# Gated linear attention on one core: the outputs of the last two heads go into spare rows of the output tiles

## The chip, the core and the metric

The kernel runs on one core of a Trainium2 chip. That core has a matrix engine (TensorE, PE in the profile; PEld is its weight load), a vector engine (VectorE, DVE), an activation engine (ScalarE, ACT), a general engine (GpSimd, POOL), and a queue engine (SyncE, SP) that in this kernel issues almost all transfers. Operands lie in SBUF, a memory of 128 partitions; the matrix engine writes to PSUM, of which this kernel uses eight banks of 128 x 512 fp32 in its later part. Inputs, outputs and spilled data lie in HBM. The metric is the device time of one execution in microseconds (us), less being better.

## What is computed

The reference, cut to what matters (2048 tokens, width 640, 32 heads of 20 features, a feed-forward width of 1536; all fp32):

```python
xn = _layernorm(x)
q, k, v = heads(xn @ wqkv)                       # 32 heads, 20 features each
phi = lambda t: concat(softmax(t @ w_phi), softmax(-(t @ w_phi)))    # 40 per head
kv = einsum("bhsf,bhsd->bhfd", phi(k), v)        # a 40 x 20 state for each head
z = einsum("bhsf->bhf", phi(k))
o = (phi(q) @ kv) / (phi(q) @ z + 1e-6)
s = o.reshape(B, S, D) @ wo
g = silu(gelu(xn @ w1 + b1) @ w2 + b2)
return x + s * g
```

## The kernel before

**Stages.** A first stage projects keys and values and sums up the state `kv`, then projects the queries. A second stage runs the feed-forward part in 12 units. A third stage, at the end, is the one that the change touches: for each of four chunks of 512 tokens (loop over `ORDER = (2, 3, 0, 1)`) it makes the attention output `o`, multiplies it by `wo`, multiplies by the gate, adds the residual and stores the result. In the second and third stage the order of the instructions on every engine is the order of the code (`manual_schedule`).

**Precision.** A large product is done in three passes on split operands (`PASSES`): a value is kept as a high part, written by ScalarE, and the low remainder, written by VectorE; high x high, high x low and low x high are added up. So a tile of outputs `oT[0][j]` has the shape 128 x 2 x 512, high part first.

**Rows of the output tiles.** Thirty heads have 600 features, which lie in five tiles `oT[0][0..4]` of 128 rows: each tile holds two groups of 60 features in 64 rows, so that 4 of every 64 rows are spare and hold zeros (`bdk`, the block-diagonal state, has 64 columns of which 60 are used). The last two heads have 40 more features. They have a tile of their own, `oT[1]`: `bdl` holds their state three times side by side (120 columns), so that one product makes three copies in 120 rows; VectorE subtracts the high part from one copy by a column of factors (`lowsel`), and `load_wol` builds a matching 120-row weight `wol` (with `midsel`). So all three passes of these 40 features are one product of 120 rows.

**Three functions of a chunk.**
- `num_t` transposes `phi(q)` of 256 tokens (half `p` of the chunk) for one tile `j` into `ph`; `j` = 5 stands for the last two heads.
- `num_m` multiplies `ph` by `bdk` or `bdl` in fp32 (two column halves of the array, each its own instruction) and splits the result into `oT`. `num_groups` does the 12 pairs (`j`, `p`) in groups of four (of three for the first chunk): transposes of a group, then the products of the group before it, then a `yield`.
- `finish(c, d, ...)` makes 128 columns (`d` = 0 to 4) of the result for a chunk: 15 products of 512 columns from `oT[0]` and a sixteenth from `oT[1]`, then the gate on VectorE and the residual sum on GpSimd (on VectorE for the last two), both in halves of 256, then the store.

**Order.** In the loop over `d`, `load_res` issues the loads of residual `xres` and gate `gt` two steps ahead, `finish` comes next, then a step of `late_q` (head sums and scaling of four query tiles, those of the chunk that comes last, each ending in a store to `phi_dram`), then one group of the next chunk's `num_groups`. So the next chunk's `oT` is made between the `finish` steps of this one: groups of transposes and products after `d` = 0, 1, 2, the last products after `d` = 3, nothing after `d` = 4. All loads and stores go through SP, which issues them in order and waits at each for what that one needs. `load_phi` loads four tiles of 640 KB; the one for the third chunk stands after `d` = 0 of the first, the one for the fourth after `d` = 3 of the second.

Of the kernel before, what the change touches and what calls it, by code (L numbers as in the profile page):

```python
# [8 lines left out]
F32 = mybir.dt.float32  # L9
F32R = mybir.dt.float32r  # L10
# [5 lines left out]
P = 128  # L16
# [29 lines left out]
def hedgehog_gated_mlp_kernel(ctx: ExitStack, tc: tile.TileContext, x, xt_in, wqk, bd, wv, wo, w1, b1, w2, b2, out_t):  # L46
# [62 lines left out]
    for h in range(3):  # L109
# [4 lines left out]
    lowsel = const.tile([P, 1], F32, name="lowsel")  # L114
    nc.gpsimd.memset(lowsel[:], -1.0)
    nc.gpsimd.affine_select(out=lowsel[:], in_=lowsel[:], pattern=[[0, 1]],
                            compare_op=OP.is_ge, fill=0.0, base=-80, channel_multiplier=1)
    midsel = const.tile([P, 1], F32, name="midsel")
    nc.gpsimd.memset(midsel[:], -1.0)
    nc.gpsimd.affine_select(out=midsel[:], in_=midsel[:], pattern=[[0, 1]],  # L120
                            compare_op=OP.is_ge, fill=0.0, base=-40, channel_multiplier=1)
    nc.gpsimd.affine_select(out=midsel[:], in_=midsel[:], pattern=[[0, 1]],
                            compare_op=OP.is_ge, fill=0.0, base=79, channel_multiplier=-1)
    const.tile([P, 8], F32, name="align")
    bdk = const.tile([P, 10, 64], F32, name="bdk")
    bdl = const.tile([P, 120], F32, name="bdl")
# [436 lines left out]
    def kv_rest():  # L563
        kv_acc(NT - 1, phis.pop(NT - 1), vs.pop(NT - 1))
        kvr = const.tile([P, 360], F32, name="kvr")
# [7 lines left out]
    def kv_state(kvr):  # L573
        nc.gpsimd.memset(bdk[:, :, 60:], 0.0)
        ps = bankB()
        for g, m in enumerate((P, P, 96)):
            nc.tensor.transpose(ps[:120, g * P:g * P + m], kvr[:m, 120 * g:120 * g + 120], ident[:m, :m])
        s3 = ps[:120, :320].rearrange("p (f r) -> p f r", r=32)
        nc.vector.tensor_tensor(bdk[:120, :, :60].rearrange("p f (h d) -> p f h d", d=20),
                                s3[:, :, None, :20].to_broadcast([120, 10, 3, 20]),  # L580
                                mask[:120, None, :, None].to_broadcast([120, 10, 3, 20]), op=OP.mult)
        for r in range(3):
            nc.vector.tensor_tensor(bdl[:80, 40 * r:40 * r + 40].rearrange("p (h d) -> p h d", d=20),
                                    ps[:80, None, 320:340].to_broadcast([80, 2, 20]),
                                    mask[:80, :2, None].to_broadcast([80, 2, 20]), op=OP.mult)
# [95 lines left out]

    def q_load(t):
        e = slab(F32, "eq")
        ef = e[:].rearrange("p a b -> p (a b)")
        nc.sync.dma_start(ef, e_dram[t])
        return ef

    def q_norm(t, ef):
# [19 lines left out]
        nc.sync.dma_start(phi_dram[t], ef)  # L708

    def load_wol():  # L710
        raw = row([P, D], F32, "raw")
        for r in range(3):
# [338 lines left out]
```

## Time and profile before

| what | value |
|---|---|
| time, median of 3 runs | 686.34 us (686.0 to 686.5) |
| the profiled execution's own time | 688.63 us |
| its span on the core | 686.9 us |
| granted TensorE clock in that span | 0.999 |
| instructions | 11941 |
| HBM read, written | 79.85 MB, 45.10 MB |

The span is the time from the first to the last instruction on the core; the execution's own time has some 1.7 us around it. Profiled and unprofiled executions differ a little, so a sum that is made on the profiled one is set against the median as a difference. In the rows below, L804 is line 804 of the kernel before; a name such as `pB<-oT,wo` says what is written from what, with buffer numbers left out. A matrix instruction in fp32 shows as two records, one in the format of the split operands as one. `busy` of matrix instructions overlaps, since they are pipelined: the distance between starts is what one costs in a row of them, and the view of the chain of work that ended last is cut at such starts.

### The profile page before, as it was taken

The numbers are of one execution on the slowest core, as the hardware profiler recorded it, in microseconds if no ns is written. First come the engines' busy times: TensorE is split into PE (matmuls) and PEld (weight loads), VectorE is DVE, ScalarE is ACT, GpSimd is POOL, SyncE is SP. The second block draws the span as 40 slices with busy tenths as digits, with TensorE's granted clock in tenths as the row PEclk, the third lists the DMA queues.
The fourth block names the chain that finished last, engine by engine and source line by source line (L and its number), as shares of the span: only waits on it lengthen the run. The fifth ranks groups of instructions, "written<-read, shape, count | busy, mean of one in ns | idle before, by whom it ended". The sixth has DMA issues, their size and how long they took to land.

```text
span 686.9 us, 11941 instructions
## 1 busy us (share of the span) xinstructions
PE 676.7 (99%) x4713; PEld 590.6 (86%) x4713; DVE 455.5 (66%) x730; ACT 251.3 (37%) x398; POOL 375.6 (55%) x336
## 2 busy tenths in 40 slices
PE   8899999999999999999999999999999999999997
PEld 8899999999999998888887888888888887777875
DVE  4788566886876456677978774676977655774232
ACT  3332313323332237244353347633233354425430
POOL 1355244859577355866968853636456640783221
PEclk9999999999999999999999999999999999999999
DMA  9820052734261153329687697376364491886623
GB/s 339 305 88 2 3 150 81 242 79 149 51 216 59 80 171 134 115 70 329 211 301 260 210 421 319 90 266 240 140 206 153 145 396 49 314 295 210 231 93 107
DMA packets 73966, 125.73 MB, mean 183 GB/s; under 512 B 5694, under 2 KB 42558, under 8 KB 73014
## 3 DMA queue, kind: packets, MB, share of 16 engines
q1 hardware_dynamic: 71606, 114.48, 48.9%
q10 hardware_dynamic: 2304, 10.49, 4.2%
q8 instruction: 37, 0.61, 0.4%
q14 instruction: 19, 0.16, 0.1%
HBM read 79.85 MB, written 45.10 MB: 182 GB/s over the span
## 4 chain that ended last, share of the span: by engine, by line
PE 90%; DVE 5%; ACT 1%; issue 1%; DMA 1%; POOL 1%; SPq 0%; DVEq 0%; POOLq 0%; ACTq 0%
PE pA L306 30%; PE pB L645 22%; PE pB L616 18%; PE pB L804 11%; PE pB L746 3%; PE pB L735 2%; PE kv L377 2%; PE pA L163 2%; DVE y L654 2%; DVE xhi L670 1%; DMA xt<-in_x_dram 1%; PE pA L292 1%; PE pB L753 1%; DVE rc L340 0%; PE pB L590 0%
## 5 line engine op out<-in xcount | busy, mean ns | idle before, releaser
L645 PE MATMUL pB<-hs,w2s 128*128 128x512 f32 x720 | 167.1, 390 | 0.0
L645 PEld LDWEIGHTS pB<-hs,w2s 128*128 128x128 f32 x720 | 134.7, 188 | 29.2 <-PE pB L746 0.8
L616 PE MATMUL pB<-xp,w1s 128*128 128x512 f32 x324 | 81.4, 390 | 1.0 <-DVE pB L888 1.0
L616 PE MATMUL pB<-xd,w1s 128*128 128x512 f32 x324 | 79.3, 389 | 0.0
L332 ACT ACTIVATE e<-e 128x1280 f32<-128x1280 f32 x32 | 40.7, 1272 | 91.5 <-POOL e L327 91.0
L804 PE MATMUL pB<-oT,wo 128*128 128x512 f32 x300 | 72.9, 394 | 0.0
L616 PEld LDWEIGHTS pB<-xp,w1s 128*128 128x128 f32 x324 | 60.7, 188 | 13.9 <-DVE pB L888 1.4
L654 DVE TENSOR_TENSOR y<-pB,y 128x512 f32<-128x512 f32 x100 | 63.9, 680 | 12.3 <-PE pB L645 12.1
L616 PEld LDWEIGHTS pB<-xd,w1s 128*128 128x128 f32 x324 | 60.8, 188 | 12.6
L804 PEld LDWEIGHTS pB<-oT,wo 128*128 128x128 f32 x300 | 55.4, 188 | 14.8 <-ACT ph L738 1.2
L345 POOL TENSOR_TENSOR e<-e,rc 128x1280 f32<-128x1280 f32 x16 | 39.0, 2440 | 48.5 <-DVE rc L365 48.2
L345 POOL TENSOR_TENSOR eq<-eq,rc 128x1280 f32<-128x1280 f32 x16 | 38.0, 2372 | 50.0 <-DVE rc L704 50.0
L327 POOL TENSOR_TENSOR e<-nr,e 128x640 f32<-128x640 f32 x32 | 45.4, 1421 | 33.5 <-DVE nr L326 30.7
L306 PE MATMUL pA<-wv,xp 128*128 128x320 f32 x384 | 61.0, 312 | 0.8 <-DVE nr L326 0.4
L621 ACT ACTIVATE pB<-pB,b1t 128x512 f32<-128x512 f32 x48 | 31.8, 662 | 77.3 <-DVE pB L888 28.4
L306 PE MATMUL pA<-wk,xp 128*128 128x320 f32 x384 | 59.9, 311 | 0.0
L306 PE MATMUL pA<-wq,xp 128*128 128x320 f32 x384 | 59.0, 309 | 0.0
L306 PEld LDWEIGHTS pA<-wv,xp 128*128 128x128 f32 x384 | 56.9, 188 | 1.7 <-issue 0.7
L306 PEld LDWEIGHTS pA<-wq,xp 128*128 128x128 f32 x384 | 56.9, 188 | 0.1
L306 PEld LDWEIGHTS pA<-wk,xp 128*128 128x128 f32 x384 | 56.8, 188 | 0.1
L691 POOL TENSOR_TENSOR ez<-eq,zrep 128x1280 f32<-128x1280 f32 x16 | 47.3, 2953 | 1.1 <-PE pB L753 1.1
L401 POOL TENSOR_TENSOR w1s<-raw,w1s 128x640 fp32r<-128x640 f32 (+1 forms) x18 | 25.7, 1429 | 36.8 <-ACT w1s L400 29.6
(139 smaller groups left out, 1046.0 us busy)
## 6 DMA issues: line engine op xcount, KB each, us to landing
raw<-in_w_dram SPq DMA_DIRECT2D x42, 320.0 KB, 4.4
e_dram<-e ACTq DMA_DIRECT2D x16, 640.0 KB, 3.3
eq<-e_dram SPq DMA_DIRECT2D x16, 640.0 KB, 6.9
phi_dram<-eq SPq DMA_DIRECT2D x16, 640.0 KB, 3.4
phi<-phi_dram SPq DMA_DIRECT2D x16, 640.0 KB, 9.5
xt<-in_x_dram SPq DMA_DIRECT2D x16, 320.0 KB, 4.8
xres<-in_xt_dram SPq DMA_DIRECT2D x20, 256.0 KB, 4.5
out_dram<-xres SPq DMA_DIRECT2D x18, 256.0 KB, 3.0
```

The lines of the kernel that those rows point to most:

```text
L306: nc.tensor.matmul(ps[:, hf, :HALF], stat_x(q, o, k, a), ws[k][:, b, hf * HALF:(hf + 1) * HALF], start=n == 0, stop=n == 3 * KC - 1)
L327: nc.gpsimd.tensor_tensor(e5[:, :, :, 1, :], nr[:, :, :, None].to_broadcast([P, 2, 16, DH]), e5[:, :, :, 0, :], op=OP.subtract)
L332: nc.scalar.activation(ef, ef, AF.Exp)
L345: nc.gpsimd.tensor_tensor(e3, e3, rc[:, :, None].to_broadcast([P, 64, DH]), op=OP.mult)
L401: nc.gpsimd.tensor_tensor(sl[:, 1, :n], src, sl[:, 0, :n].bitcast(F32), op=OP.subtract)
L616: nc.tensor.matmul(bank[ch][:], tl[:, a, off + wo_:off + wo_ + P], mov(blk, b), start=new and n == 0, stop=n == len(mms) - 1, skip_group_c ...
L621: nc.scalar.activation(ps, ps, AF.Gelu_apprx_tanh, bias=b1t[:, f:f + 1])
L645: nc.tensor.matmul(ps[:], ws[i][:, b, d * P:(d + 1) * P], hs[o][i][:, a, :], start=i == n == 0, stop=(i, n) == (GF - 1, 2), skip_group_che ...
L654: nc.vector.tensor_tensor(y, ps[:], y, op=OP.add)
L691: nc.gpsimd.tensor_tensor(zv, ef, zf, op=OP.mult)
L746: nc.tensor.matmul(po[64 * e:64 * e + 64, :256], bdk[:n, 2 * j + e, :], ph[:n, e * 256:(e + 1) * 256], start=True, stop=True)
L804: nc.tensor.matmul(ps[:], w, o, start=n == 0, stop=n == 15)
```

## The change

The 40 outputs of the last two heads are now moved into the 4 spare rows of every 64: rows 15, 31, 47, ... of each tile `oT[0][j]`, eight rows for each of the five tiles. `bdk`'s columns, and the rows of `wo` on the host, are put in the order that leaves every sixteenth row free, and `wo` has 640 rows in place of 680. `bdl` has 40 columns, made by one instruction; `lowsel`, `midsel` and `load_wol` are gone. A transfer from SBUF to SBUF (`spread`) copies eight rows of `oT[1]` (high and low part of 512 tokens, 4 KB a row) into `oT[0][j]` behind the products of the second half of `j`; to that end `j` = 5 is done first. `finish` has fifteen products. The residual sum of all steps is on VectorE, in one piece of 512 columns (halves in the last two steps). In the chunk loop, stores are collected and issued after the step's products (`put`, `put_all`), and the fourth chunk's `load_phi` stands after `d` = 2 of the second chunk.

```diff
-    bdl = const.tile([P, 120], F32, name="bdl")
+    bdl = const.tile([P, 40], F32, name="bdl")
...
-        nc.vector.tensor_tensor(bdk[:120, :, :60].rearrange("p f (h d) -> p f h d", d=20),
-                                s3[:, :, None, :20].to_broadcast([120, 10, 3, 20]),
-                                mask[:120, None, :, None].to_broadcast([120, 10, 3, 20]), op=OP.mult)
-        for r in range(3):
...
+        for h in range(3):
+            nc.vector.tensor_scalar(
+                bdk[:120].rearrange("p f (q c) -> p f q c", c=16)[:, :, :, 5 * h:5 * h + 5],
+                s3[:, :, :20].rearrange("p f (q i) -> p f q i", i=5), mask[:120, h:h + 1], None, op0=OP.mult)
...
+    stores, late_store = [], [False]
+
+    def put(dst, src):
+        if late_store[0]:
+            stores.append((dst, src))
+        else:
+            nc.sync.dma_start(dst, src)
+
+    def put_all():
+        while stores:
+            nc.sync.dma_start(*stores.pop(0))
...
-            for a, b in ((0, 64), (64, 120)):
-                nc.tensor.matmul(po[a:b, :256], bdl[:n, a:b], ph[:n, :256], start=True, stop=True)
+            nc.tensor.matmul(po[:40, :256], bdl[:n, :], ph[:n, :256], start=True, stop=True)
             o2 = oT[1]
...
+    def spread(j, oT):
+        nc.sync.dma_start(oT[0][j][15::16].bitcast(F32), oT[1][8 * j:8 * j + 8].bitcast(F32))
...
-        steps = [(j, p) for p in range(2) for j in range(6)]
+        steps = [(j, p) for p in range(2) for j in (5, 0, 1, 2, 3, 4)]
...
+                num_m(j, oT, p, n, ph)
+                if p and j < 5:
+                    spread(j, oT)
...
-        steps.append((wol[:120, d * P:(d + 1) * P], oT[1][:120, 1, :]))
         for n, (w, o) in enumerate(steps):
-            nc.tensor.matmul(ps[:], w, o, start=n == 0, stop=n == 15)
+            nc.tensor.matmul(ps[:], w, o, start=n == 0, stop=n == 14)
...
-        for o in range(2):
-            sl = slice(o * W2, (o + 1) * W2)
+        w = W2 if last else CW
+        for o in range(0, CW, w):
+            sl = slice(o, o + w)
...
-            (nc.vector if last else nc.gpsimd).tensor_tensor(xr[:, sl], g, xr[:, sl], op=OP.add)
+            nc.vector.tensor_tensor(xr[:, sl], g, xr[:, sl], op=OP.add)
...
-            nc.sync.dma_start(out_t[d * P:(d + 1) * P, c * CW:(c + 1) * CW], xr[:])
+            put(out_t[d * P:(d + 1) * P, c * CW:(c + 1) * CW], xr[:])
...
-    wol = load_wol()
...
             next(nxt, None)
-            if ci + 2 < NCH and d == (0 if ci == 0 else 3):
+            put_all()
+            if ci + 2 < NCH and d == 2 * ci:
                 phin = load_phi(ORDER[ci + 2])
```

What the change moves is seen best in the order of instructions on two engines. **SP, in the first chunk's steps `d` = 2 and 3**; first before (`out_0_dram` is the result, `eq` a query tile of `late_q`, `phi_dram` its store):

```order
L784 DMA xres_6064<-in_xt_dram 128x512
L788 DMA gt_6066<-g_dram_86 128x512
L814 DMA out_0_dram<-xres_5907 128x512
L708 DMA phi_dram_82<-eq_5935 128x1280
L784 DMA xres_6147<-in_xt_dram 128x512
L788 DMA gt_6149<-g_dram_86 128x512
L814 DMA out_0_dram<-xres_5984 128x512
L685 DMA eq_6173<-e_dram_81 128x1280
```

and the same place now:

```order
L781 DMA xres_6043<-in_xt_dram 128x512
L785 DMA gt_6045<-g_dram_86 128x512
L749 DMA oT_5889<-oTl_5894 8x1024
L683 DMA out_0_dram<-xres_5895 128x512
L781 DMA xres_6124<-in_xt_dram 128x512
L785 DMA gt_6126<-g_dram_86 128x512
L688 DMA eq_6146<-e_dram_81 128x1280
L749 DMA oT_5890<-oTl_5894 8x1024
L749 DMA oT_5891<-oTl_5894 8x1024
L749 DMA oT_5892<-oTl_5894 8x1024
L749 DMA oT_5893<-oTl_5894 8x1024
L683 DMA phi_dram_82<-eq_5919 128x1280
```

The small transfers of the next chunk's tiles (`oT<-oTl`) stand between loads and stores; four of them come in a row behind two loads and a query tile, and the store of the step's result stands behind them.

**SP, in the second chunk's steps `d` = 2 and 3**, before:

```order
L784 DMA xres_6379<-in_xt_dram 128x512
L788 DMA gt_6381<-g_dram_86 128x512
L814 DMA out_0_dram<-xres_6244 128x512
L784 DMA xres_6451<-in_xt_dram 128x512
L814 DMA out_0_dram<-xres_6306 128x512
L725 DMA phi_6496<-phi_dram_82 128x1280
L725 DMA phi_6497<-phi_dram_82 128x1280
```

and now:

```order
L785 DMA gt_6348<-g_dram_86 128x512
L749 DMA oT_6214<-oTl_6219 8x1024
L683 DMA out_0_dram<-xres_6220 128x512
L716 DMA phi_6417<-phi_dram_82 128x1280
L716 DMA phi_6418<-phi_dram_82 128x1280
L716 DMA phi_6419<-phi_dram_82 128x1280
L716 DMA phi_6420<-phi_dram_82 128x1280
L781 DMA xres_6425<-in_xt_dram 128x512
L749 DMA oT_6215<-oTl_6219 8x1024
L749 DMA oT_6216<-oTl_6219 8x1024
L749 DMA oT_6217<-oTl_6219 8x1024
L749 DMA oT_6218<-oTl_6219 8x1024
```

The four tiles of `phi` are now issued one step earlier, and the four small transfers stand right behind them.

**VectorE, around the last products of the first chunk's loop** (step `d` = 3; `rc` and `dn` are head sums of `late_q`), before:

```order
L809 TENSOR_TENSOR gt<-pB,gt 128x256 x2
L340 TENSOR_REDUCE rc<-eq 128x64
L694 RECIPROCAL rc<-rc 128x64
L750 TENSOR_TENSOR oT<-pB,oT 128x256 x3
L756 SCALAR_TENSOR_TENSOR oTl<-oTl,lowsel,pB 120x256
L340 TENSOR_REDUCE dn<-ez 128x64
```

and now:

```order
L806 TENSOR_TENSOR gt<-pB,gt 128x512
L807 TENSOR_TENSOR xres<-gt,xres 128x512
L330 TENSOR_REDUCE rc<-eq 128x64
L697 RECIPROCAL rc<-rc 128x64
L741 TENSOR_TENSOR oT<-pB,oT 128x256 x4
L330 TENSOR_REDUCE dn<-ez 128x64
```

The residual sum stands ahead of the head sum, and four low parts of `oT` follow behind it in place of three and the copy of the last two heads.

More of the change, by code (lines that the diff above doesn't have):

```diff
@@ L707, in q_norm @@
         yield
[L708 to L712, printed above, removed]
-            nc.sync.dma_start(raw[40 * r:40 * r + 40, :], wo[640:680, :])
-        wol_h = row([P, D], F32R, "wolh")
-        wol = row([P, D], F32R, "wol")
-        nc.vector.tensor_copy(wol_h[:120, :], raw[:120, :])
-        nc.vector.scalar_tensor_tensor(wol[:120, :], wol_h[:120, :].bitcast(F32), midsel[:120, :], raw[:120, :],
-                                       op0=OP.mult, op1=OP.add)
-        return wol
+        put(phi_dram[t], ef)
     def load_phi(c):
```

46 lines of the change are left out of this document (18 added, 28 removed).

## The prediction

> **What bounds the kernel now.** I read the page's busy times and its chain first, then the chain of the last 150 us in order of time, then the engines' busy times by stage.
>
> ```profile
> PE 676.7 (99%) x4713; PEld 590.6 (86%) x4713; DVE 455.5 (66%) x730; ACT 251.3 (37%) x398; POOL 375.6 (55%) x336
> PEclk9999999999999999999999999999999999999999
> PE 90%; DVE 5%; ACT 1%; issue 1%; DMA 1%; POOL 1%; SPq 0%; DVEq 0%; POOLq 0%; ACTq 0%
> ```
>
> The matrix engine is busy 99% of the span, at full clock in every slice, and 90% of the chain is its work. The change touches the third stage; of its chain from 540 us on I need the shares and these pieces (start, length, what):
>
> ```profile
> by line: PE pB L804 50.1%; PE pB L746 12.9%; PE pB L645 12.3%; PE pB L735 9.1%; PE pB L616 8.2%; PE pB L753 2.3%; DVE xres L810 0.6%; DVE y L809 0.5%; issue 0.1%; DVEq L809 0.0%
> ...
> 579.68 3.63 PE pB L804 x16
> ...
> 601.92 1.45 PE pB L746 x12
> 603.36 0.43 PE pB L753 x4
> 603.80 7.51 PE pB L804 x32
> ...
> 626.06 3.86 PE pB L804 x16
> ...
> 631.80 7.51 PE pB L804 x32
> ...
> 659.99 22.14 PE pB L804 x96
> ...
> 682.22 0.44 DVE y L809
> ```
>
> By the first row the chain from 540 us on has hardly an engine but PE, and what others have of it stands at the end: from 682 us the last gate and sum, then the store. What is taken off the matrix engine in this stage is gained, unless something then makes it wait.
>
> **The sixteenth product.** In the row of 659.99, 96 products of 512 columns take 22.14 us, back to back: 0.2306 us each. `finish` runs 20 times (4 chunks, 5 steps) and loses one product each time: 20 x 0.2306 = **4.61 us**, all on the path.
>
> **The halved product of the last two heads.** `num_m` with `j` = 5 runs 8 times (4 chunks, 2 token halves) and has one instruction of 40 columns in place of two of 64 and 56. To see what that is worth I need the price of such a record when it runs alone. L590 has fp32 records over the whole array:
>
> ```profile
> 267.84 2.15 PE pB L590 x8
> L590 PE MATMUL pB<-kvr,ident x8: 366/448/466, 267.7 to 269.6; 128*128 128x360 f32 x4, 128*128 128x320 f32 x2, 128*128 128x240 f32 x2
> ```
>
> 4 x 360 + 2 x 320 + 2 x 240 = 2560 columns in 2.15 us, or 0.215 us for 256 columns. The four records of L753 (two instructions, two records each) take 0.43 us, half of 4 x 0.215, so the two column halves run side by side. One instruction alone is then 2 x 0.215 = 0.43 us, as long as the pair. I take **0**. Were a record worth 0.108 us whatever stands beside it, two fewer would give 8 x 0.215 = 1.7 us; if the odd one also keeps its neighbours of L746 from pairing, up to as much is lost. The Trainium skill, "TensorEngine Tiling (Array Packing)", section Tiling Modes, says that different tiles of the array can run matrix instructions in parallel; by it nothing is saved here, without it 1.7 us, and the two rows agree with it.
>
> **VectorE and GpSimd.** 18 of the 20 steps change: two gate products of 256 on VectorE and two sums on GpSimd become one product and one sum of 512 on VectorE.
>
> ```profile
> L809 DVE TENSOR_TENSOR y<-pB,y 128x256 f32<-128x256 f32 x20 | 7.7, 420 | 29.5 <-PE pB L804 29.5
> L654 DVE TENSOR_TENSOR y<-pB,y 128x512 f32<-128x512 f32 x9 | 6.1, 690 | 2.5 <-PE pB L645 2.5
> L810 POOL TENSOR_TENSOR xres<-gt,xres 128x256 f32<-128x256 f32 x20 | 14.3, 737 | 27.7 <-DVE gt L809 22.5 <-issue 5.1
> 580.00:600.00 20.00, 20.00 (x132) 15.83 (x131) 12.52 (x24) 8.16 (x20) 12.38 (x9) 1.00 0.70 250
> 600.00:610.00 10.00, 10.00 (x52) 7.49 (x51) 8.55 (x19) 1.54 (x4) 7.67 (x6) 1.00 0.84 300
> 620.00:630.00 10.00, 10.00 (x62) 7.58 (x62) 3.52 (x11) 5.31 (x11) 4.57 (x5) 1.00 0.66 204
> ```
>
> GpSimd loses 36 x 0.737 = 26.5 us, which stood on no path. VectorE pays 2 x 0.690 - 2 x 0.420 = 0.54 us more per step. In the last rows (columns PE, PEld, DVE, ACT, POOL, clock, DMA share, GB/s) VectorE is busy 12.5 of 20 us and 3.5 of 10, which hides this; but from 600 to 610 it has only 1.45 us left, because the head sums of `late_q` run there. So the cover is thin in the first chunk's loop alone: 5 x 0.54 = 2.7 us there, if it were gone. `load_wol` leaves VectorE, and `kv_state` has four small instructions as before, of other shapes; the feed-forward products (L645) run beside both and nobody waits for them, so they count nothing, and 1 us at most (two of the 0.690 row) if `kv_state`'s were slower and waited for.
>
> **The small transfers.** `spread` is new, and it adds a wait: the first products of `finish` on tile `j` need its transfer landed, which needs the low half of `oT` from VectorE and SP's queue. Products `j` begin at 3`j` x 0.2306 us into `finish`. No row shows a transfer of 32 KB inside SBUF; the nearest ones:
>
> ```profile
> out_dram<-xres SPq DMA_DIRECT2D x4, 128.0 KB, 1.9
> st_dram<-pst SPq DMA_DIRECT2D x4, 2.0 KB, 3.0
> 585.32 0.34 SPq L814 DMA_DIRECT2D out_dram<-xres  x1
> xres<-in_xt_dram SPq DMA_DIRECT2D x3, 256.0 KB, 8.1
> DMA to landing us min/median/max: 5.5/9.5/11.7
> ```
>
> An issue keeps SP for 0.34 us; the smallest transfers land 1.9 to 3.0 us after it. With much queued ahead it is worse: 8.1 us for 256 KB between 565 and 600 us, and up to 11.7 us for a `phi` tile (last row). I take 2 to 3 us on a quiet queue, and go through the four places where an `oT` is finished.
>
> *First chunk.*
>
> ```profile
> 577.70 0.86 DVE L750 TENSOR_TENSOR oT<-pB,oT 128x256 fp32r<-128x256 f32 x2 [0.32 <-ACT oT L749]
> ```
>
> The last low halves, now `j` = 2, 3, 4, come at about 578.1, 578.5 and 579.0; with issue and 1.9 to 3.0 us they land at 580.3 to 581.4, ..., 581.2 to 582.3. `finish` starts at 579.68 and needs them at 581.06, 581.75 and 582.45. Wait: 0, at most 0.4 us.
>
> *First to second chunk.* The last products end at 603.80.
>
> ```profile
> 603.78 1.49 DVE L340 TENSOR_REDUCE rc<-eq 128x64 f32<-128x1280 f32 x1 [1.07 <-DMA eq<-e_dram]
> 605.78 1.02 DVE L750 TENSOR_TENSOR oT<-pB,oT 128x256 fp32r<-128x256 f32 x3
> ```
>
> Three low halves end at 606.80, because a head sum (and its reciprocal) goes ahead of them that waited 1.07 us for a query tile. Now the step's gate and sum ahead of it take 0.6 us more. Without that wait (GpSimd and the stores are earlier, so the tile's load is too) the four low halves come 1.9 to 3.1 us after the products, with it 3.0 to 4.1 us. The transfers land 2.2 to 3.3 us later: `j` = 1 at 4.1 to 6.3 us, `j` = 4 at 5.3 to 7.4 us. The step between takes 15 x 0.2306 = 3.46 us, so `j` = 1 is needed at 4.15 and `j` = 4 at 6.23. Wait: 0 to 2.2 us; I take 0.8, nearer to the low end, as the load's wait should go.
>
> *Second to third chunk.* Here 4 x 640 KB of `phi` go onto the queue one step earlier, right ahead of the transfers.
>
> ```profile
> L750 DVE TENSOR_TENSOR oT<-pB,oT 128x256 fp32r<-128x256 f32 x40 | 15.1, 417 | 9.0 <-ACT oT L749 7.2 <-PE pB L746 1.7
> L749 ACT ACTIVATE oT<-pB 128x256 fp32r<-128x256 f32 x40 | 13.7, 392 | 11.0 <-PE pB L746 10.7
> 623.57 1.67 SPq L708 DMA_DIRECT2D phi_dram<-eq  x1
> 632.30 2.13 SPq L725 DMA_DIRECT2D phi<-phi_dram  x4
> 639.35 1.27 PEld L735 LDWEIGHTS pB<-identr,phi 128*120 128x120 f32 x15 [0.29 <-DMA phi<-phi_dram]
> ```
>
> Before, they were issued from 632.30 and the matrix engine still waited for them at 639.35, 7.05 us later. In the new order they follow `j` = 0's transfer and the store of `d` = 2. The products of `j` = 0 end at 626.06, its high half takes 0.39 and its low half 0.42 us, so `phi` starts at about 627.8 and lands at 634.9. (It also needs the last `phi_dram` store, issued at 623.57, 4 us ahead of the load.) The transfers of `j` = 1 to 4 are issued at 632.3 to 633.5 and land, if they queue behind, at about 636; `j` = 1 is needed at 631.80 + 4.15 = 635.95. Wait: 0 to 3 us (the upper end by the 9.5 us median of a `phi` tile); I take 0.4. The 0.29 us that waited for `phi` goes.
>
> *Third to fourth chunk.* The queue holds one residual tile and one store. Wait: 0.
>
> ```profile
> SPq L814 <- POOL xres L810: 36.2, 9, 14.8
> ```
>
> SP waited 36.2 us (580 to 640) for GpSimd's sums at the head of its queue; that goes, and waits of `spread` for VectorE come. Behind these stand stores, the residual and gate of two steps ahead and a query tile, which nobody needs for the next 3.5 us. A store that is put behind the step's products keeps its residual row some 2 us longer, of which a row is free now that `wol` is gone. Behind a product that waits for its transfer stands all of PE's queue, so such a wait counts in full.
>
> **Sum.** -4.61 + 0 + 0 + 0.8 + 0.4 = -3.4 us. The profiled execution took 688.63 us (span 686.9 and 1.7 around it), so 685.2 for it; the median of the runs shown is 2.3 us lower, 686.34, so **682.9 us**.
>
> **Rivals.**
> - *The queue.* The small transfers wait behind all that SP issued ahead of them. If at the first boundary they land as slowly as the 8.1 us row, `j` = 1 comes at 1.9 + 0.3 + 8.1 = 10.3 for 4.15, a wait of 6.1 us; if at the second they take a `phi` tile's 11.7 us from 632.3, 644.0 for 635.95, another 8.1 us. Together 686.34 - 4.61 + 14.2 = 695.9 us. It decides for slower from 6 us of waits in all. For it: DMA share 0.84 from 600 to 610. Against: at both places the loads ahead were issued 2 us or more earlier, and at the second `phi` should be through when `j` = 1 is needed. The Trainium skill, "DMA: Bandwidth & Descriptors", section on queues, rings and completion order, says that one engine takes a queue's descriptors in ring order, which is this rival's rule; no row of a small transfer behind a large one is here to test it.
> - *VectorE becomes the bound* in the first chunk's loop: its 2.7 us come onto the path beside the 1.2 of waits: 686.34 - 4.61 + 3.9 = 685.6 us. For it: 8.55 of 10 us busy. Against, the row below: three of its waits, 4.3 us, were for GpSimd's product of queries and sums, which no longer stands behind GpSimd's residual sums.
> ```profile
> DVE dn L340 <- POOL ez L691: 4.3, 3, 2.1
> ```
>
> - *The halved product pays* after all: 682.9 - 1.7 = 681.2 us.
> - *The sixteenth product was hidden* and the change does nothing: 686.3. Against: 96 products at an even 0.2306.
>
> **How the numbers follow.** Forecast 0.64 (681.5 to 685), halved product 0.12, VectorE 0.14, queue 0.08, nothing 0.02. About 0.2% (1.4 us) is what a measurement tells from no change here. Faster: 0.64 + 0.12 = 0.76; same: 0.14 + 0.02 = 0.16; slower: 0.08. The range goes from 681.0 (halved product) to 686.0 (VectorE, or waits at their upper ends), and leaves out the queue and the edges.
>
> **What would show it.** L804's successor has 300 records in rows of 0.2306 us per product, and the last six steps' 96 become 90 in 20.8 us. `bdl`'s two records take 0.43 us. In the chain, gaps of PE ahead of the second and third chunk's first `finish` are the waits, released by DMA `oT<-oTl`; landing times of these tell 2 to 3 us from 8. If VectorE is the bound, PE waits for it (L806, L741), not for a DMA. I am wrong if these waits sum to more than 3 us, or if the gap between the last product and the end grows.

## The result, and the profile after

The changed kernel takes **691.58 us** (median of 4 runs, 691.09 to 692.47) where the kernel before takes 686.4 (686.0 to 686.5): a ratio of 1.0078, 95% interval [1.0061, 1.0095]. It is slower by 5.2 us; the forecast was 3.4 us faster. The profiled execution after took 691.87 us, with a span of 689.8. That is only 2.9 us longer than the 686.9 of the profile before, because the profiled execution before had lost some 2.4 us ahead of the third stage: the first product of `finish` started at 579.68 us there and starts at 577.32 now.

In the rows of the changed kernel L800 is a product of `finish`, L806 its gate and L807 its sum, L737 and L743 the products of `num_m` (L743 those of the last two heads), L726 the transposes of `num_t`, L749 `spread` and L716 `load_phi`; in some of the runs a line number is a little off from these.

The page of the changed kernel, its rows of busy times, of the granted clock in 40 slices and of the chain's shares:

```profile
PE 673.7 (98%) x4677; PEld 588.3 (85%) x4677; DVE 464.3 (67%) x728; ACT 251.4 (36%) x398; POOL 351.8 (51%) x295
PEclk9999999999999999999999999999999999999899
PE 93%; DMA 3%; DVE 2%; issue 1%; POOL 1%; ACT 0%; SPq 0%; POOLq 0%; DVEq 0%
```

The matrix engine has 36 records fewer and 3 us less to do, yet the span is longer: one slice near the end is below full clock, and the chain now has 3% of transfers. The next rows are the only places after 594 us where the matrix engine's timeline shows idle time, with its cause in brackets; behind them stand pieces of the chain (start, length, what), and the windows of ten microseconds around the second place (columns: length, busy time of PE, PEld, DVE, ACT, POOL, clock, DMA share, GB/s).

```profile
607.13 3.00 PE L800 MATMUL pB<-oT,wo 128*128 128x512 f32 x12 [2.31 <-DMA oT<-oTl]
639.75 5.02 PE L800 MATMUL pB<-oT,wo 128*128 128x512 f32 x12 [5.53 <-DMA oT<-oTl]
```
```profile
602.39 4.61 DMA oT<-oTl
...
630.02 9.60 DMA oT<-oTl
...
664.58 20.64 PE pB L800 x90
```
```profile
630.00:640.00 10.00, 4.47 (x19) 3.43 (x20) 2.21 (x5) 1.58 (x3) 0.00 (x0) 0.86 0.83 312
640.00:650.00 10.00, 10.00 (x52) 8.24 (x53) 1.90 (x3) 2.73 (x6) 0.00 (x0) 0.79 0.32 93
```

Both waits are for the new transfers, at the second and the third chunk's first `finish` (the first and the second boundary from here on): 2.31 and 5.53 us. After the longer one, twelve products take 5.02 us where 12 x 0.2293 = 2.75 is the price at full clock (90 take 20.64): the clock in the last two rows is 0.86 and 0.79, and another **2.3 us** are lost behind the wait. Behind the first wait, at a clock of 1.00, the twelve took 3.00 us, so about 2.0 of the 2.3 are the clock's. With the 4.6 us of the sixteenth product the profiled third stage comes out at about -4.6 + 2.3 + 5.5 + 2.3 = +5.5 us; from the first product of `finish` to the last it grew from 102.45 to 107.89 us.

Three questions follow. Is `finish` with fifteen products really worth 4.6 us? Why do transfers of 32 KB take 4.6 and 9.6 us? And is VectorE, which took over the sums, part of it?

### The profile page after: what moved, and what is told of

It reads as the page before. It is cut to its first block, busy times and chain, and to the rows that moved or that the text cites. A ratio compares the mean times of both kernels' runs of the same rounds, so it can differ in the third digit from the quotient of the medians.

```text
span 689.8 us, 11833 instructions
## 1 busy us (share of the span) xinstructions
PE 673.7 (98%) x4677; PEld 588.3 (85%) x4677; DVE 464.3 (67%) x728; ACT 251.4 (36%) x398; POOL 351.8 (51%) x295
## 4 chain that ended last, share of the span: by engine, by line
PE 93%; DMA 3%; DVE 2%; issue 1%; POOL 1%; ACT 0%; SPq 0%; POOLq 0%; DVEq 0%
PE pA L296 30%; PE pB L636 24%; PE pB L607 21%; PE pB L800 9%; PE pB L737 2%; DMA oT<-oTl 2%; PE pB L726 2%; PE kv L367 2%; PE pA L153 2%; DMA xt<-in_x_dram 1%; PE pA L282 1%; PE pB L743 1%; DVE xres L807 0%; PE pB L581 0%; POOL e L317 0%
## 5 line engine op out<-in xcount | busy, mean ns | idle before, releaser
L800 PE MATMUL pB<-oT,wo 128*128 128x512 f32 x300 | 74.3, 403 | 7.8 <-DMA oT<-oTl 7.8
L800 PEld LDWEIGHTS pB<-oT,wo 128*128 128x128 f32 x300 | 56.8, 193 | 23.7 <-issue 8.6
```

What stands on the lines that cost most here:

```text
L800: nc.tensor.matmul(ps[:], w, o, start=n == 0, stop=n == 14)
```

## The experiments

### The product alone, and the transfers left out

`e5_product_only` is the kernel before with the sixteenth product removed, so it leaves the last two heads out of the result:

```diff
-        steps.append((wol[:120, d * P:(d + 1) * P], oT[1][:120, 1, :]))
...
-            nc.tensor.matmul(ps[:], w, o, start=n == 0, stop=n == 15)
+            nc.tensor.matmul(ps[:], w, o, start=n == 0, stop=n == 14)
```

> The kernel before with one edit alone: each of the 20 steps stops at its fifteenth product, so the last two heads are left out of the result; their outputs are still made, the sums stay on GpSimd, nothing is transferred. If the sixteenth product is worth its 0.23 us each time and nothing else ends the steps, 686.3 - 4.6 = 681.7 us (681.4 to 682.0), the matrix engine never waiting more than 0.3 us in the last 110 us. If the steps of before were held by GpSimd or VectorE as well, less is gained: 683 to 685, with the wait named there. Theory of the transfers and theory of VectorE both need 681.7 here, since both say that the fifteen products alone are no trouble.

Measured: 681.7 us (681.38 to 682.57), ratio 0.9929 [0.9915, 0.9944]. The product is worth its price: 686.66 in the same series less 681.7 is 5.0 us for a forecast of 4.6. The matrix engine waits for nothing in the last 110 us, so nothing else held the steps of before. 681.7 is the floor against which the rest is read.

`e1_no_transfer` is the changed kernel without `spread`; it too leaves the last two heads out:

```diff
-                if p and j < 5:
-                    spread(j, oT)
```

> The changed kernel without the small transfers: the 40 outputs of the last two heads never reach the output tiles, so they are left out of the result. Theory 'queue' (the loss is the matrix engine's wait for these transfers, and the half clock behind the longer wait): what is left is the removed products, 20 x 0.23, so 686.4 - 4.6 = 681.8 us, no gap ahead of any output step, clock 1.0 throughout. Theory 'VectorE' (the sums moved to it make the low halves late): the steps wait for the low halves even now, 684 us or more. If the halved product had a price or a gain of its own, the time would be off 681.8 by up to 1.7 us either way.

Measured: 684.19 us (680.97 to 686.34, 10 runs), ratio 0.9964 [0.9947, 0.998]. No wait for a transfer is left, so the transfers carry most of the loss; but 2.5 us over the floor remain, and runs lie 5 us apart. Its timeline, VectorE and then GpSimd (`ez` is GpSimd's product of queries and sums):

```profile
599.12 3.41 DVE L805 TENSOR_TENSOR xres<-gt,xres 128x512 f32<-128x512 f32 x1
```
```profile
599.04 2.93 POOL L694 TENSOR_TENSOR ez<-eq,zrep 128x1280 f32<-128x1280 f32 x1
```

A sum that elsewhere takes 0.69 us takes 3.41 when GpSimd's product started 0.08 us ahead of it: the remaining 2.85 us of GpSimd's product, and 0.56 more. By these times VectorE did next to nothing until GpSimd was done. In the changed kernel the same is to be seen in the group of its first ten sums (busy time, mean ns) beside the eight of the later steps, where GpSimd has nothing left to do:

```profile
L807 DVE TENSOR_TENSOR xres<-gt,xres 128x512 f32<-128x512 f32 x10 | 11.9, 1189 | 0.4
L807 DVE TENSOR_TENSOR xres<-y,xres 128x512 f32<-128x512 f32 x8 | 5.5, 692 | 0.3
```

The ten cost 11.9 us, 5.0 more than ten times 0.69. The Trainium skill, "SBUF — State Buffer", section "SBUF: two separate sides", says that VectorE and GpSimd share one pair of ports, locked for a whole instruction, and that VectorE needs it when both inputs lie in SBUF and GpSimd reads SBUF too. The rows agree, and the next two runs test it.

### The sum reads PSUM

`e6_sum_psum` leaves the gate product in its bank, so that the sum has one operand in SBUF; `e7_no_transfer_psum` does the same to `e1_no_transfer` (and leaves out what that leaves out):

```diff
-            nc.vector.tensor_tensor(g, ps[:, sl], g, op=OP.mult)
-            nc.vector.tensor_tensor(xr[:, sl], g, xr[:, sl], op=OP.add)
+            nc.vector.tensor_tensor(ps[:, sl], ps[:, sl], g, op=OP.mult)
+            nc.vector.tensor_tensor(xr[:, sl], ps[:, sl], xr[:, sl], op=OP.add)
```

> The changed kernel, with the gate product written back into its PSUM bank and the residual sum reading it from there, so that VectorE's sum has one operand in SBUF in place of two. Theory of the shared port (a sum with two SBUF operands waits for a GpSimd product that reads SBUF): no sum is longer than 0.8 us, where 2.2 to 2.4 us were seen; the low parts come up to 1.7 us earlier in the first chunk's loop, the wait for the first transfers (2.3 us) shrinks to under 1, the wait behind the phi loads (5.5 us) stays, as does the slow clock after it: about 689.5 to 690 us. If stretched sums only fill VectorE's idle time, 691.6 as before this edit. If the transfers at the first boundary are slow in themselves (4.6 us to land), the wait there stays at 2 us and the time within 691 to 692.

> The run without transfers (outputs of the last two heads left out of the result), with the sum reading PSUM as in the run ahead. That run took 684.2 us where 681.8 was to be had, with a spread of 5 us. Theory of the shared port: the sums of 3.4 us beside GpSimd's products were what held VectorE; now all sums are under 0.8 us, the matrix engine waits for no low part and its clock stays at 1.0, so 681.8 us with a spread under 1. If VectorE has simply too much to do in the first chunk's loop (two head sums of 1.5 us in each step beside the 0.69 us product and sum), it stays at 684 and goes on waiting for low parts.

Measured: `e7_no_transfer_psum` 681.84 us (681.18 to 681.94), ratio 0.9927 [0.9913, 0.9942], the floor, and steady. `e6_sum_psum` 689.92 (688.92 to 690.78), ratio 1.0047 [1.0032, 1.0062], 1.7 us better than the changed kernel. The sums in the group view of `e6_sum_psum`, and its two waits on the matrix engine's timeline:

```profile
L807 DVE TENSOR_TENSOR xres<-pB,xres 128x512 f32<-128x512 f32 x18 | 12.4, 691 | 0.7
```
```profile
604.83 3.00 PE L800 MATMUL pB<-oT,wo 128*128 128x512 f32 x12 [0.34 <-DMA oT<-oTl]
637.34 4.42 PE L800 MATMUL pB<-oT,wo 128*128 128x512 f32 x12 [5.41 <-DMA oT<-oTl]
```

All eighteen sums take 0.69 us, and the first wait falls from 2.31 to 0.34 us. How a stretched sum got into a transfer is seen in SP's timeline, first of the changed kernel, then of `e6_sum_psum`:

```profile
598.21 0.58 SPq L749 DMA_DIRECT2D oT<-oTl  x1
...
600.31 0.42 SPq L688 DMA_DIRECT2D eq<-e_dram  x1
602.39 2.57 SPq L749 DMA_DIRECT2D oT<-oTl  x4
```
```profile
596.87 0.58 SPq L749 DMA_DIRECT2D oT<-oTl  x1
...
598.97 0.42 SPq L688 DMA_DIRECT2D eq<-e_dram  x1
602.06 2.56 SPq L749 DMA_DIRECT2D oT<-oTl  x4
```

The first small transfer waits at the head of SP's queue for a low half from VectorE. There VectorE is 1.34 us earlier in `e6_sum_psum`, so the residual, the gate and the 640 KB query tile (`eq`) behind that transfer go out 1.34 us earlier too. The four other transfers go out at nearly the same time in both, and land 4.61 and 2.63 us later: 6.7 and 5.7 us after the query tile's issue. So VectorE's delay seems to have come back as traffic in front of the transfers; no run moved the query tile alone. The wait behind the phi loads hardly changed: 5.41 us.

`e4_sum_pool` asks the opposite: the sums go back to GpSimd, the rest stays as changed.

```diff
-            nc.vector.tensor_tensor(xr[:, sl], g, xr[:, sl], op=OP.add)
+            (nc.vector if last else nc.gpsimd).tensor_tensor(xr[:, sl], g, xr[:, sl], op=OP.add)
```

> The residual sums go back to GpSimd, in one piece of 512 columns; all else as changed. Theory 'queue': the low halves come 0.7 us earlier at both places, but the transfers still land behind the loads: 691 us, within 1 us of the changed kernel. Theory 'VectorE': the first wait of 2.3 us goes, 689 us or less.

Measured: 695.4 us (694.32 to 696.56), ratio 1.013 [1.0114, 1.0145]; both theories missed, by 4 us and more. The matrix engine's two waits there:

```profile
609.27 4.42 PE L800 MATMUL pB<-oT,wo 128*128 128x512 f32 x12 [3.91 <-DMA oT<-oTl]
643.90 5.46 PE L800 MATMUL pB<-oT,wo 128*128 128x512 f32 x12 [6.12 <-DMA oT<-oTl]
```

The sum then stands behind GpSimd's products, and SP, in order, holds its stores for it (26.9 us of waits at the head of its queue between 565 and 668 us), so both waits grow. The sum's move to VectorE is itself worth 3.8 us beside the transfers; it is the two SBUF operands that spoil part of it.

### The clock behind the wait

`e8_fill` puts 24 products whose results are overwritten where the matrix engine waits longest:

```diff
-    def finish(c, d, oT, last):
+    def finish(c, d, oT, last, fill=None):
         ps = bankB()
+        for n in range(24 if fill else 0):
+            nc.tensor.matmul(ps[:], wo_s[0][:, 0, :P], fill[0][0][:, 0, :], start=True, stop=True)
...
-            finish(c, d, oT, ci == NCH - 1 and d >= 3)
+            finish(c, d, oT, ci == NCH - 1 and d >= 3, oTp if ci == 2 and d == 0 else None)
```

> The changed kernel with 24 further products of 512 columns (5.5 us) on operands that lie there already, written into the bank of the third chunk's first step ahead of its own products, which overwrite them; nothing reads them. They stand where the matrix engine waited 5.5 us for the transfer behind the phi loads. Theory of the clock: what follows the wait was slow because the engine had been idle; kept busy, the clock stays at 1.0 there, twelve products take 2.8 in place of 5.0 us, and the time falls by the 2.2 us to about 689.4 although 24 products were added. If the slow stretch has another cause (the products wait for the later transfers one by one), the 5.0 us stay and the time is 691.6 or more.

Measured: 689.21 us (688.84 to 690.31), ratio 1.0042 [1.0028, 1.0056]. More work, 2.4 us less time. Its chain there, and its windows:

```profile
632.72 5.44 PE pB L799 x24
638.16 3.59 PE pB L802 x15
```
```profile
630.00:640.00 10.00, 10.00 (x45) 8.03 (x45) 1.39 (x3) 0.75 (x2) 0.00 (x0) 1.00 0.83 314
640.00:650.00 10.00, 10.00 (x69) 8.04 (x68) 3.93 (x8) 5.78 (x14) 0.00 (x0) 1.00 0.35 108
```

The fill takes as long as the wait did, all fifteen products behind it take 3.59 us, and the clock is 1.00 throughout. So the slow products came from the idle time. The Trainium skill, "TensorE: Matmul & The Clock Gate", section "Part 1: The HAM clock gate", says that the clock is halved after an idle window of some 3.4 us that runs freely; the trace agrees, with 0.50 in each window of 2 us from 638 to 644 us, after a wait of 5.53 us, and 1.00 where the wait was filled.

### Where the transfers wait

`e2_phi_behind` puts the fourth chunk's phi load one step later, behind the transfers:

```diff
-            if ci + 2 < NCH and d == 2 * ci:
+            if ci + 2 < NCH and d == 3 * ci:
```

> The fourth chunk's phi loads one step later, as before the change, so that the small transfers of that place stand ahead of them. Theory 'queue': the second wait (5.5 us) and the half clock behind it (2.25 us) go; phi is then late itself, by about 3 us for the transposes that follow; 691.6 - 7.8 + 3 = 686.8 us. The first wait (2.3 us) stays. Theory 'slow transfer' (a transfer inside SBUF takes this long whatever stands ahead): the second wait stays, 691 us or more. Theory 'VectorE': nothing changes, 691.6 us.

Measured: 689.49 us (689.27 to 691.65), ratio 1.0051 [1.0033, 1.0068]. From its chain and from the matrix engine's timeline:

```profile
633.60 7.49 DMA phi<-phi_dram
```
```profile
639.69 0.23 PE L726 MATMUL pB<-identr,phi 128*80 128x128 f32 x1 [2.58 <-DMA phi<-phi_dram]
641.14 1.77 PE L726 MATMUL pB<-identr,phi 128*80 128x128 f32 x13 [1.22 <-DMA phi<-phi_dram]
```

The second wait for the transfers is gone, the first stays (2.13 us), and 3.8 us of waits for phi stand in the second's place. The forecast of 686.8 took 3 us for them and nothing behind them; but thirteen transposes take 1.77 us there, where fourteen take 1.08 elsewhere, and the clock is 0.50 from 642 to 644 us. Two loads compete for the same few microseconds, and either order loses.

`e3_act_queue` issues the transfers from ScalarE's queue, behind the products of their group:

```diff
-        nc.sync.dma_start(oT[0][j][15::16].bitcast(F32), oT[1][8 * j:8 * j + 8].bitcast(F32))
+        nc.scalar.dma_start(oT[0][j][15::16].bitcast(F32), oT[1][8 * j:8 * j + 8].bitcast(F32))
...
                 num_m(j, oT, p, n, ph)
+            for j, p, n, ph in group:
                 if p and j < 5:
                     spread(j, oT)
```

> The small transfers are issued from ScalarE's queue, a group of them behind its products; nothing else changes. Theory 'queue': they no longer stand behind the loads, land 2 to 3 us after their issue, and both waits go, the first but for what VectorE makes late (0 to 1 us): 691.6 - 2.3 - 5.5 - 2.25 = 681.6, up to 683 us. Theory 'slow transfer' (the 16 DMA engines are full, so that any queue is slow): 689 to 692 us. Theory 'VectorE': the first wait stays, 684 us.

Measured: 688.25 us (687.93 to 690.5), ratio 1.0033 [1.0021, 1.0044]; no theory had this number. At the first boundary a transfer landed in 2.80 us, but a sum of 3.41 us had made it late (a wait of 3.22 us); at the second the matrix engine waited 1.16 us for a gate from ScalarE, which had spent 4.54 us on four issues. The run mixes three effects and decides nothing alone.

`e10_early` and `e12_early2_psum` leave the queue alone and move the first group of the next chunk's transposes one step ahead, so that two steps lie between the transfers and their use; the second does it at both boundaries and takes the sum from PSUM.

```diff
...
             next(nxt, None)
+            if ci == 0 and d == 4:
+                o = new_oT(late)
+                pend = (num_groups(phin, o), o)
+                next(pend[0])
             put_all()
```

> The changed kernel with the third chunk's first group of transposes one step earlier, in the last step of the first chunk's loop, so that in the second chunk's loop the last products and their transfers come after d = 2 and two steps (6.9 us and a group of nothing else) lie between them and their use; the phi load of the fourth chunk stays after d = 2 and so stands behind the transfers. Theory of the queue: the transfers land in 2 to 4.6 us, the 5.5 us wait and the slow clock after it (2.25 us) go, the 2.3 us wait at the first boundary stays: 691.6 - 7.8 = 683.8 us, up to 1.5 more if the transposes then wait for phi. Theory that the transfers are slow whatever stands ahead of them (9.6 us from issue to landing): still 2 us or more of wait there and 686 to 688.

> Both remedies at both boundaries: the sum reads PSUM, and the first group of transposes of the second and of the third chunk stands one step earlier, so that each set of transfers has two steps of 3.5 us before its use. If the transfers' lateness, the stretched sums and the clock are the whole loss, nothing waits for a transfer and the time is that of fifteen products, 681.7 to 682.2 us. If VectorE or the matrix engine's waits for phi take over, 683 to 685, with that wait in the last 110 us.

Measured: `e10_early` 685.28 us (681.96 to 686.53), ratio 0.9968 [0.9951, 0.9985], the forecast's 683.8 with the 1.5 that phi might add, though single runs lie 4.6 us apart; `e12_early2_psum` 686.37 (684.65 to 688.07), ratio 0.9997 [0.9985, 1.0008], 4 us above its forecast. In `e10_early` the wait behind the phi load is gone as expected, 1.54 us for phi came, and 1.12 us are left of the first wait. The second was a miss; its chain, and the matrix engine's wait:

```profile
603.96 6.45 DMA eq<-e_dram
```
```profile
613.88 1.12 PE L737 MATMUL pB<-ph,bdk 120*64 120x256 f32 x4 [2.37 <-DVE xres L807]
```

Here the transfers stand ahead of a query tile that VectorE needs for its head sums; the tile comes late, VectorE behind it, and the matrix engine waits for a bank, with a clock of 0.84 between 600 and 620 us. As with phi: what is put ahead of the queue makes late what stood there.

### Phi on other queues

Four runs start from `e6_sum_psum`. `e13_phi_pool` issues the fourth chunk's phi load from GpSimd's queue, `e14_phi_act` from ScalarE's:

```diff
-    def load_phi(c):
+    def load_phi(c, q=nc.sync):
...
-            nc.sync.dma_start(tl[i][:].bitcast(F32), phi_dram[TPC * c + i])
+            q.dma_start(tl[i][:].bitcast(F32), phi_dram[TPC * c + i])
...
-                phin = load_phi(ORDER[ci + 2])
+                phin = load_phi(ORDER[ci + 2], nc.gpsimd if ci else nc.sync)
```

> The run with the sum from PSUM (689.9 us), and the fourth chunk's phi load issued at the same place of the program from GpSimd's queue in place of SP's: same bytes, same moment, another ring. Theory of the ring order (a small transfer waits for what was issued ahead of it on its own queue): the four transfers land in 2 to 4 us in place of 9.5, the 5.4 us wait goes and with it the slow clock (some 1.6 us there): 683 to 684 us. Theory of full DMA engines (2.6 MB of phi keep all of them busy, whatever the queue): the transfers still land 7 us or more after issue, the wait stays at 3 to 5 us, and the time is 687 to 690.

> As the run with the phi load on GpSimd's queue, but from ScalarE's queue, where it stands behind the high halves of d = 2's products. In the run on GpSimd's queue three of the four phi tiles went out at 617.8 us, nine earlier than before, since that queue had no stores to wait for, so it does not tell a transfer's place in the ring from full DMA engines. Here phi goes out at about 628 us, just ahead of the transfers and in flight with them. Theory of the ring order: the transfers, first in their own ring, land 2 to 4.5 us after issue, the matrix engine waits under 1.5 us for them, its clock stays at 1.0, and the time is 683 to 685 us (ScalarE loses 2.3 us to the four issues). Theory of full DMA engines: they land 7 us or more after issue, the wait is 3 to 5 us, and the time 687 to 690.

Measured: `e13_phi_pool` **683.0 us** (682.72 to 685.57, 6 runs), ratio 0.9954 [0.9939, 0.9968]; `e14_phi_act` 685.67 (683.89 to 687.81), ratio 0.9984 [0.9971, 0.9996]. GpSimd's timeline in `e13_phi_pool`, and a piece of its chain:

```profile
617.82 1.81 POOL L716 DMA_DIRECT2D phi<-phi_dram  x3
622.20 0.54 POOL L716 DMA_DIRECT2D phi<-phi_dram  x1 [2.56 <-DMA phi_dram<-eq]
```
```profile
627.88 4.41 DMA oT<-oTl
```

This run beat both kernels, but not for the reason that was expected: GpSimd's queue had none of the step's stores ahead of the load, and three tiles went out 6.5 us earlier than in `e6_sum_psum` (8.8 us earlier than in the changed kernel). The waits for transfers are 0.54 and 0.19 us. In `e14_phi_act` the tiles are in flight with the transfers, and time and wait lie between its two forecasts; its ScalarE timeline, its chain, its wait, and the DMA queues between 628 and 632 us (q10 carries phi, q1 what SP issued):

```profile
623.08 2.47 ACTq L716 DMA_DIRECT2D phi<-phi_dram  x4
```
```profile
628.48 6.93 DMA oT<-oTl
```
```profile
635.54 4.50 PE L800 MATMUL pB<-oT,wo 128*128 128x512 f32 x12 [2.71 <-DMA oT<-oTl]
```
```profile
q10 hardware_dynamic: 244, 1.10, 69.6%
q1 hardware_dynamic: 204, 0.39, 25.0%
```

A queue of its own did not free the transfers: phi took 70% of the engines' time. One residual load still stood ahead of them, so `e15_phi_act_res` and `e16_phi_pool_res` move that load behind them, the first on top of `e14_phi_act`, the second of `e13_phi_pool`:

```diff
-            load_res(ci * KC + d + 2)
+            if ci > 1 or d != 3:
+                load_res(ci * KC + d + 2)
...
             put_all()
+            if ci < 2 and d == 3:
+                load_res(ci * KC + d + 2)
```

> The run with phi on ScalarE's queue (685.7 us, transfers landing 6.9 us after issue), with one more edit: in the first and second chunk's step d = 3 the loads of a residual (and gate) are issued behind the four transfers in place of ahead of them. Phi is still in flight when the transfers are issued, on another ring. Theory of the ring order: nothing large stands ahead of them in their own ring, so they land 2 to 4 us after issue although phi is in flight; no wait over 0.5 us, 683 to 684.5 us (ScalarE still pays for the issues). Theory of shared DMA engines: they land 5.5 us or more after issue, the wait of 1.5 to 2.7 us stays, and the time is 685 to 686.5.

> The run with phi on GpSimd's queue (683.0 us), with the same edit: residual and gate loads of step d = 3 behind the transfers in the first and second chunk. Theory of the ring order: at the second boundary nothing is ahead of the transfers, which land in 2 to 2.5 us in place of 4.4; at the first only the query tile's 640 KB are, and they land in 2 to 2.5 us as well; no wait for a transfer over 0.3 us: 682.0 to 682.6 us, and steadier than 682.7 to 685.6. If the place in the ring counts for nothing there, 683.0 with waits of 0.2 to 0.5 us as before; if the residuals now come late, VectorE waits for them and the time is 683 to 684.

Measured: `e15_phi_act_res` 684.19 us (683.84 to 686.75), ratio 0.9973 [0.9961, 0.9986]; `e16_phi_pool_res` 683.81 (682.43 to 684.3), ratio 0.9962 [0.9947, 0.9977]. From `e15_phi_act_res`, the last three issues of phi, a store ahead of the transfers, and the transfers' landing:

```profile
622.98 1.70 ACTq L716 DMA_DIRECT2D phi<-phi_dram  x3
```
```profile
624.30 1.33 SPq L683 DMA_DIRECT2D out_dram<-xres  x1
```
```profile
627.97 5.81 DMA oT<-oTl
```

In the last 3.6 us ahead of them only a store of 256 KB is issued on their queue, and they still take 5.81 us. The expectation of 2 to 4 us fell: landing and wait (1.58 us) are those of the theory of shared engines, though the time, 684.19, lies in the range of the other. In `e16_phi_pool_res` they take 5.58, no better than the 4.41 of `e13_phi_pool` (the matrix engine waits 1.36 us for them); VectorE waits 3.91 us for the gate tile that was moved back, the matrix engine 0.43 us for VectorE. The same two views, of issues and of the chain, for the changed kernel and for `e6_sum_psum` and `e16_phi_pool_res`:

```profile
626.59 2.32 SPq L716 DMA_DIRECT2D phi<-phi_dram  x4
```
```profile
624.29 2.28 SPq L716 DMA_DIRECT2D phi<-phi_dram  x4
```
```profile
627.70 9.50 DMA oT<-oTl
```
```profile
623.77 0.54 POOL L716 DMA_DIRECT2D phi<-phi_dram  x1 [2.55 <-DMA phi_dram<-eq]
```
```profile
628.23 5.58 DMA oT<-oTl
```

Side by side, start and length added up (of the four transfers, the one that the matrix engine waited for):

| run | phi from | last phi issue ends | transfers land | after their own issue | after phi's last |
|---|---|---|---|---|---|
| changed kernel | SP | 628.91 | 639.62 | 9.60 | 10.7 |
| `e6_sum_psum` | SP | 626.57 | 637.20 | 9.50 | 10.6 |
| `e14_phi_act` | ScalarE | 625.55 | 635.41 | 6.93 | 9.9 |
| `e15_phi_act_res` | ScalarE | 624.68 | 633.78 | 5.81 | 9.1 |
| `e13_phi_pool` | GpSimd | 622.74 | 632.29 | 4.41 | 9.6 |
| `e16_phi_pool_res` | GpSimd | 624.31 | 633.81 | 5.58 | 9.5 |

The time from the transfers' own issue varies from 4.4 to 9.6 us; the time from phi's last issue stays between 9.1 and 10.7, whichever queue carries phi and whatever stands ahead of the transfers in theirs. Where phi has a queue of its own, its end can be seen: its last bytes move between 632 and 633 us in `e13_phi_pool` (the transfers land at 632.29) and between 634 and 635 in `e14_phi_act` (635.41); in `e15_phi_act_res` and `e16_phi_pool_res` 0.05 and 0.02 MB of it still move from 634 to 635, after the landings at 633.78 and 633.81. So the transfers land when phi is through or all but through. The ring order, the theory that I held up to here, explains little of it. The Trainium skill, "DMA: Bandwidth & Descriptors", section "Issuing engines are not separate DMA queues", says that transfers of all queues run on the same 16 engines and interleave there, and that another queue saves only the time to issue; the table agrees. Of the 2.6 us by which the transfers of `e14_phi_act` land sooner after their issue than those of `e6_sum_psum`, 1.0 is an earlier phi and 0.8 a later issue of their own. How the engines share themselves between the queues was not tried by itself and stays open; that all are full can't be the whole of it, since in the changed kernel their busy share is 0.35 from 638 to 639 us and the transfers land only at 639.62.

## Why the prediction was wrong

- **The sixteenth product: right.** -4.61 forecast; 90 products take 20.64 us, and it alone gives 686.66 - 681.7 = 5.0 us.
- **The halved product: right.** No gain was forecast. In the changed kernel's chain the lone records (L743) push their neighbours (L737) out of step:

```profile
586.38 0.34 PE pB L743
586.72 0.03 PE pB L737
586.75 0.18 PE pB L743
586.94 1.30 PE pB L737 x11
```

  Together 1.85 us, where 12 + 4 records took 1.45 + 0.43 before.
- **Second to third chunk: the step that failed most.** It took `phi` from its issue to 7.05 us later, and put the transfers' landing at "about 636" for a need at 635.95. The 7.05 us is the time until the first waiting transposes could run, not until four tiles were through. The transfers landed at 639.62, 13.0 us after phi's first issue where 8.2 was forecast, for a need at 639.75 - 5.53 = 634.22. Forecast wait 0.4, measured 5.53. The better row was there: the 9.5 us median of a `phi` tile, counted from phi's last issue, gives 627.8 + 2.1 + 9.5 = 639.4; it was used for the upper end alone.
- **The clock was not in the sum at all.** A wait was priced at its length; 5.53 us cost 2.3 more behind it, of which about 2.0 are the clock's, and `e8_fill` gave back 2.4.
- **First to second chunk: 0.8 forecast, 2.31 measured.** The low halves came in time: the transfers were issued 1.9 us after the products, as forecast. The landing was taken as 1.9 to 3.0 us and was 4.61, behind a query tile issued 2.1 us ahead. "At both places the loads ahead were issued 2 us or more earlier" was the reason against the queue rival; 2.1 and 3.4 us earlier were not enough.
- **VectorE: the cover was there, the price was not.** 0.54 us a step was forecast, from two rows without GpSimd beside them. The first ten sums cost 5.0 us more, by waiting for GpSimd.
- **The rivals.** The queue rival, at a chance of 0.08 and 695.9 us, had the right place and the right sign; its cause, the order within one queue, was not borne out. The bound for being wrong, waits over 3 us, was passed with 7.8.

The loss adds up over runs that differ by one or two edits each: 681.84 with neither transfers nor stretched sums (`e7_no_transfer_psum`); 683.0 with transfers and phi out early (+1.2); 689.92 with phi just ahead of the transfers, its slow clock included (+6.9); 691.58 with the sums reading two SBUF operands (+1.7). So the saving of the product is real, and the transfers need not cost more than 1.2 of it: `e13_phi_pool`, which leaves nothing out, takes 3.7 us less than the kernel before.

## What to carry to other kernels

In these runs a small transfer was as late as the large ones in flight with it, on whichever queue: behind 2.6 MB of phi it landed 9.1 to 10.7 us after phi's last issue. Before putting one on the path, look at what is issued in the ten microseconds ahead of it, and move that earlier rather than behind. Price a wait of the matrix engine with the clock behind it, here up to 2 us. When an elementwise sum moves from GpSimd to VectorE while GpSimd still works, keep one operand in PSUM: the sums took 0.69 us so, and up to 3.41 with both in SBUF.

## What was not expected of the hardware

- VectorE's sum of two SBUF operands took 3.41 in place of 0.69 us beside a GpSimd product; the other way round, GpSimd's `ez` took 3.42 in place of 2.93 when VectorE's sum had started 0.09 us ahead of it.
- A transfer of 32 KB within SBUF landed 2.3 us after its issue at best (`e10_early`), and up to 9.6 behind 2.6 MB of phi in the changed kernel; one issue kept SP for 0.58 us, where a store of 256 KB took 0.34.
- 24 useless products made the kernel 2.4 us faster.
- Whether the clock falls behind a wait can't be told from the wait's length alone. The windows of the changed kernel around its 2.31 us wait, then those of `e1_no_transfer` around a wait of 1.94 us for VectorE at 621.42:

```profile
605.00:615.00 10.00, 7.87 (x47) 6.65 (x48) 8.61 (x13) 1.95 (x4) 5.28 (x2) 1.00 0.89 290
```
```profile
620.00:630.00 10.00, 8.58 (x43) 5.55 (x45) 6.04 (x13) 4.73 (x10) 0.48 (x1) 0.83 0.86 284
```

  The longer one left the clock at 1.00, the shorter one took it to 0.83 (0.57 and 0.58 in the two windows of 2 us from 622 on). The Trainium skill, "TensorE: Matmul & The Clock Gate", section "Part 1: The HAM clock gate", names an idle window of some 3.4 us as what halves the clock; here 1.94 us were enough, so page and run differ. That the 5 us between runs of `e1_no_transfer` come from this is likely and was not shown.
